# Recurrent attention and routed experts on one core: the state in compact form, its turning and routing rearranged

## The chip, the cores and the metric

The kernel runs on one core of a Trainium2 chip. The metric is the time of one execution on the device in microseconds (us). A core has five engines, each with a queue of its own that it works off in order: TensorE (PE, with its weight loads PEld), VectorE (DVE), ScalarE (ACT), GpSimd (POOL) and SyncE (SP), which issues DMAs. Engines wait for each other by semaphores.

## The reference

There are two parts. The first is a recurrence over 768 steps for each of 4 x 8 heads of width 40. The second sends each of the 3072 rows to one of 8 experts, by a hash of its token.

```python
for t in range(S):
    y[:, :, t] = einsum('bhd,bhde->bhe', rt, state)
    Sa = einsum('bhde,bhe->bhd', state, at)
    state_decay = state * wt[:, :, None, :] - einsum('bhd,bhe->bhde', Sa, bt)
    state = state_decay + einsum('bhd,bhe->bhde', vt, kt)
x = y.transpose(0, 2, 1, 3).reshape(3072, 320)
expert_idx = token_ids * 2654435761 % 8
out[mask_e] = maximum(x[mask_e] @ w1[e], 0) @ w2[e]
```

All is in fp32.

## The kernel before

**Tiling.** The sequence is cut into 12 chunks of 64 steps. A tile u is one chunk n of one group g of two batches with their 8 heads, so there are 24 tiles, u = 2 n + g. Inside a chunk the recurrence is solved with matrices: the products of a, b, k, r with running products of the decays w, and the inverse of a triangular matrix. Two halves of 64 partitions hold two heads (`par`) or the two batches (`be`), and four pairs of heads (`hp`) lie side by side. `quarters()` runs over hp, par and be, 16 matmuls in all, most of them of 64x64.

**Order.** `at_tick(tick, step)` collects every step as a function with a due time, in ticks; `STEPS` gives the fraction of a tick to the named steps. The plan is sorted by due time and issued in that order under a manual schedule, so each engine's program follows it. In tick T the kernel finishes tile T - 8 (`tile_b`, t0 = u + 8) and prepares tile T (`tile_a`). Ticks 8 to 31 are thus the main part; from tick 24 on there is nothing left to prepare.

**One tick, in TensorE's order.** Names are those of the PSUM tiles in the profile.
- c: r1 by the inverse um; ScalarE copies it to cv. u: the lower block of the next tile's inverse. rc, in two parts: cv by r and v by r, which VectorE masks into mr; between them nc, which turns cv; ScalarE copies it into `x_all`.
- z: turns the decayed b and k of tile T; ScalarE copies it to z_t. s: the state, in which two products with `ident` bring the old state in and 16 products add the chunk; VectorE multiplies the sum by the chunk's decay `pend` into sc, written twice (once for each head of a pair, with zeros in the other half, so that 128 rows hold a pair).
- a: the products of a with b and k; ScalarE copies them to nk and its lower part once more (L546). sd: turns sc; ScalarE copies it. x: the first half of the lower block of the inverse; ScalarE copies it to xi.
- r (r0, the state by a), t (at_t, which turns a of the next tile), r (r1, v by the masked products), y (state by r and z by mr; VectorE multiplies by the decays py into xs, and GpSimd's queue stores xs to x_rows), and t again (rv, which turns r and v).

**Groups.** For four tiles at a time VectorE inverts the 32x32 diagonal blocks (`group_i`): it transposes nk to nb, does 31 pairs of operations (L600 and L603, "outer" and "ub"), and transposes the result to ut (L608) and ug (L614). ScalarE fills ub at the start (L582).

**Decays.** For four tiles at a time `decays` builds the running products of w: clamp, chains on GpSimd, own, an exchange over TensorE, ends, a reciprocal, two spreading multiplies, transpositions pt and qt, and `pend`.

**PSUM.** `psum` hands out two large buffers in turn (tags psa0 and psa1), `bank` two small ones (psb0, psb1); ub takes the rest. A step that asks for a buffer waits until the buffer's last reader is done.

**Routing and experts.** `routing()` is a generator whose pieces are due every 0.42 tick from tick 11.5 on: it loads the token ids, counts and ranks them on VectorE, scatters token numbers to their slots (24 indirect DMAs by GpSimd), reads the slots back (idx_all, five DMAs by SyncE) and bounds them (src_all). After the last tick come the experts: gathers of x_rows, two matmul layers, scatters to out.

Of the kernel before, what the change touches and what calls it, by code (L numbers as in the profile page):

```python
# [18 lines left out]
def kernel(  # L19
# [98 lines left out]
    taken = [0, 0]  # L118

    def turn_of(i):  # L120
        taken[i] += 1
        return taken[i] % 2
# [25 lines left out]
    STEPS = ["c", "u", "rcc", "nc", "rcv", "z", "s", "a", "sd", "x", "r0", "at_t", "r1", "y", "rv"]  # L148
# [39 lines left out]
    x_all = hold.tile([P, 3, 2, HP, P], F32, name="x_all")  # L188
# [4 lines left out]
    sd_r = ring("sd", NG, [R, 2, HP, 2, D], all_of)  # L193
    sc_r = ring("sc", NG, [R, 2, HP, 2, C], all_of)
    pend_r = ring("pend", NR, [P, RN, NG, 2, HP, 2], all_of, NR)
    nk = hold.tile([P, LAG, 2, 2, HP, C], F32, name="nk")
    xi_r = ring("xi", 1, [P, H, C])
# [9 lines left out]

    @at_tick(-8.95)
    def _():
        for be in range(2):  # L210
            rows = slice(be * C + BLK, (be + 1) * C)
            nc.scalar.copy(xi_r(0)[rows, :, BLK:C], ident[rows, rows].unsqueeze(1).to_broadcast([BLK, H, BLK]))
# [30 lines left out]

    def paced(dma):

        dep = mybir.DependencyInfo(mybir.DependencyClass.Sync, mybir.DependencyReason.SCHED_ONLY)
        tc.add_manual_dep(dma.ins, pe_last[0].name, dep)
# [32 lines left out]
    def decays(ri, t_load, t_clamp, t_chain, t_own, t_ex, t_ends, t_pair, t_recip, t_en, t_spread, t_turn):  # L280
# [3 lines left out]
        chain = nc.vector if fast else nc.gpsimd  # L284

        for i in range(4 * RN):
            @at_tick(t_load + (0.06 * i if ri > 2 else 0))
            def _(i=i):
# [6 lines left out]
                eng = nc.scalar if fast and n % 2 else nc.sync  # L295
                r0 = (y * RN + n) * NG * H
                dma = eng.dma_start(x["pb"][r0:r0 + NG * H], src)
# [11 lines left out]
        def own():  # L309
            p, q = segs(x["pb"]), segs(x["qb"])  # L310
            x["own"] = own = work.tile([P, SEG, D], F32, tag="own", name="own", bufs=2)
            nc.vector.tensor_tensor(own[:], p[:, :, SL - 1], q[:, :, SL - 1], op=OP.mult)
            for s in range(SEG - 2, -1, -1):
                nc.vector.tensor_tensor(own[:, s], own[:, s], own[:, s + 1], op=OP.mult)
# [17 lines left out]
        def ends():  # L332
            ends = x["ends"]
            nc.vector.tensor_tensor(ends[:, 0:SEG], x["own"][:], ends[:, SEG].unsqueeze(1).to_broadcast([P, SEG, D]), op=OP.mult)
# [103 lines left out]
        def _():  # L438
# [3 lines left out]
            for par in range(2):  # L442
                rows = half(par)
                for be in range(2):
                    nc.scalar.copy(t[rows, :, :, be, :, par],
                                   p[rows].rearrange("p (be y n g hp two) -> p be y n g hp two", be=2, y=2, n=RN, g=NG, two=2)[:, be, 0, :, :, :, par])

    def tile_a(u):
# [19 lines left out]
        else:  # L468
            t_in, t_inz, t_mul, t_mulz = u - 1.36, u - 1.1, u - 0.6, u - 0.55
            t_z, t_at, t_a = (u - i + STEPS.index(n) / len(STEPS) for i, n in ((0, "z"), (1, "at_t"), (0, "a")))  # L470
            if u == LAG:
                t_at, t_mul, t_mulz, t_z, t_a = u + 0.66, u - 0.36, u + 0.225, u + 0.55, u + 0.79
# [59 lines left out]
        def _():  # L532
# [9 lines left out]
            if u > GRP - 2:  # L542
                nc.scalar.copy(both, p[:])  # L543
                for be in range(2):
                    low = slice(be * C + BLK, (be + 1) * C)
                    nc.scalar.copy(nk[low, u % LAG, :, 0, :, 0:BLK], p[low, :, 0:HP * C].rearrange("p two (hp t) -> p two hp t", hp=HP)[..., BLK:])  # L546
# [24 lines left out]
    def group_i(gi, t0, t1, t2, t3):  # L571
# [39 lines left out]
        def _():  # L611
            ub = x["u"]
            x["ug"] = ug = work.tile([P, BLK, BLK], F32, tag="ug", name="ug", bufs=1)
            nc.vector.transpose(ug[:].rearrange("p g t -> p t g"), ub[:].rearrange("p s t -> p t s"))  # L614
# [5 lines left out]
    def tile_m(u, t0):  # L620
# [5 lines left out]
        def _():  # L626
# [7 lines left out]
            for be in range(2):  # L634
                low = slice(be * C + BLK, (be + 1) * C)
                nc.scalar.copy(xi[low, :, 0:BLK], p[low])

        @at_tick(t0 - 1, "u")
        def _():
            ug, xi = groups[gi]["ug"], x["xi"]  # L640
            p = bank([P, H, BLK], "u_ps")
            for hp, par, be in quarters():
                h = hx(par, hp)
                low = slice(be * C + BLK, (be + 1) * C)
                mm(p[half(be), h, :], xi[low, h, :], ug[low, ti * H + h, :])
            x["um"] = um = work.tile([P, H, C], F32, tag="um", name="um", bufs=1)
            nc.scalar.copy(um[:, :, BLK:C], p[:])

        @at_tick(t0 - 0.7 if u else t0 - 0.93)
        def _():  # L650
            nc.scalar.mul(x["um"][:, :, 0:BLK], groups[gi]["ug"][:, ti * H:(ti + 1) * H, :], first[:, 0:1])

    def tile_s(u, t0):
# [5 lines left out]
        def in_rv(i):  # L659
            kind, be = divmod(i, 2)  # L660
            if i == 0:
                x["r"], x["x"] = r_r(u), x_all[:, u % 3]
# [3 lines left out]
        for i in range(4):  # L666
            @at_tick(5.0 + 0.2 * u if u < 2 else t0 - 1.84 + 0.09 * i)
# [12 lines left out]
        def _():  # L680
            x["rt"] = rv[:, :, 0]
            p = psum("t_ps")
# [548 lines left out]
```

## Time and profile before

| what | value |
|---|---|
| three runs, median (lowest, highest) | 708.71 us (699.46, 709.13) |
| the profiled execution | 702.85 us, its span 701.1 us |
| busy: PE, DVE, POOL, ACT | 606.5, 357.3, 269.2, 262.8 us |
| experts, from 432 us on | 269.0 us, PE busy 246.59 |
| L600 and L603, the pairs of the inversion | 62.7 and 65.0 us, 186 each |
| L738 mr, x24 | 1218 ns each |
| L765 sc, x22 | 819 ns each |
| L499 on POOL, 128x320, x40 | 872 ns each |
| L910 scatters to slots, x24 | 1027 ns each |

The busy time of an engine is a sum over the whole span. A line of the chain or of the timeline has the start, the duration, the engine and what ran; in the timeline the bracket at the end has the idle time ahead of the instruction and what ended it. A fp32 matmul appears as two records.

### The profile page before, as it was taken

Reading aid. Unit: us, or ns where it says so; the run is one execution under the profiler, and the core shown is the slowest. Engines: PE = TensorE matmul, PEld = TensorE weight load, DVE = VectorE, ACT = ScalarE, POOL = GpSimd, SP = SyncE. Lnnn points to the kernel's source line nnn. Section 1 sums busy time; section 2 is a strip of 40 time slices with the busy share of each in tenths; the row PEclk is TensorE's granted clock in tenths of the full one; section 3 lists DMA queues with packets and bytes.
Section 4 is the critical chain, followed back from the end, with each engine's and each line's share of the span. In section 5 each row is a group of like instructions: output and inputs, shape, how many; then the busy total and the mean of one; then the engine's idle time right before and its main releaser. Section 6 shows DMA issues by size and latency. Waiting matters only on the chain.

```text
span 701.1 us, 23965 instructions
## 1 busy us (share of the span) xinstructions
PE 606.5 (87%) x10442; PEld 455.0 (65%) x10442; DVE 357.3 (51%) x759; ACT 262.8 (37%) x520; POOL 269.2 (38%) x343
## 2 busy tenths in 40 slices
PE   0446678989999999989989994899999999999995
PEld 0335657877878888878878884364656556565653
DVE  6969797858988966873676313328111111111110
ACT  2576434754566657555534541111111111111110
POOL 2569367574637785454331111312213030210101
PEclk9988568997999999998989998699999999999999
DMA  9874053554555756774434522896322442120000
GB/s 136 157 114 113 2 105 78 116 123 91 110 110 114 133 101 102 131 136 66 80 55 82 117 55 73 297 339 217 102 73 87 145 149 85 46 93 20 28 5 29
DMA packets 163517, 73.86 MB, mean 105 GB/s; under 512 B 136078, under 2 KB 157135, under 8 KB 163408
## 3 DMA queue, kind: packets, MB, share of 16 engines
q1 hardware_dynamic: 153232, 55.55, 36.6%
q0 software_dynamic: 5824, 15.75, 8.4%
q10 hardware_dynamic: 4352, 0.98, 1.2%
q8 instruction: 83, 1.36, 0.9%
q14 instruction: 26, 0.21, 0.1%
HBM read 56.73 MB, written 12.16 MB: 98 GB/s over the span
## 4 chain that ended last, share of the span: by engine, by line
PE 39%; issue 33%; DVE 12%; POOL 6%; DMA 5%; SPq 2%; ACT 1%; POOLq 0%; DVEq 0%; ACTq 0%
PE r_ps L242 5%; PE y_ps L242 5%; PE s_ps L242 5%; PE rc_ps L242 4%; PE u_ps L242 4%; DVE ub L603 3%; DVE outer L600 3%; POOL out_dram L1030 3%; PE sd_ps L562 3%; PE a_ps L242 2%; PE z_ps L562 2%; POOL xg L1000 2%; PE t_ps L567 2%; PE nc_ps L747 2%; PE x_ps L242 2%
## 5 line engine op out<-in xcount | busy, mean ns | idle before, releaser
L1040 PE MATMUL dn_ps<-w,ht 128*128 128x320 f32 x384 | 104.9, 433 | 0.0
L1030 POOL DMA_INDIRECT out_dram<-o,idx_all x26 | 25.7, 990 | 185.4 <-ACT o L1029 178.6
L1020 PE MATMUL up_ps<-xt,w 128*128 128x416 f32 x256 | 94.0, 520 | 0.0
L1040 PEld LDWEIGHTS dn_ps<-w,ht 128*128 128x128 f32 x384 | 72.8, 190 | 32.1 <-issue 2.4
L1020 PEld LDWEIGHTS up_ps<-xt,w 128*128 128x128 f32 x256 | 47.5, 191 | 46.0 <-issue 46.0
L785 POOL DMA_DIRECT2D x_rows<-xs x44 | 24.5, 561 | 115.6 <-DVE xs L782 77.1
L603 DVE TENSOR_TENSOR ub<-ub,outer 128x31 f32<-128x31 f32 (+15 forms) x186 | 65.0, 349 | 6.3
L600 DVE TENSOR_TENSOR outer<-ub,nb 128x31 f32<-128x31 f32 (+15 forms) x186 | 62.7, 337 | 7.4 <-ACT ub L583 2.8
L1023 DVE TENSOR_SCALAR ht<-up_ps 128x416 f32<-128x416 f32 x32 | 18.9, 591 | 92.4 <-PE up_ps L1020 92.4
L1006 DVE COPY xt<-xg_ps 128x384 f32<-128x384 f32 x24 | 12.1, 551 | 83.4 <-PE xg_ps L1005 83.4
L562 PE MATMUL z_ps<-ident,z_all 128*128 128x128 f32 x192 | 32.0, 318 | 24.0 <-POOL z_all L499 10.7
L1029 ACT COPY o<-dn_ps 128x320 f32<-128x320 f32 x24 | 10.2, 426 | 101.6 <-PE dn_ps L1040 101.6
L738 DVE TENSOR_TENSOR mr<-rc_ps,after 128x1024 f32<-128x1024 f32 x24 | 29.2, 1218 | 29.3 <-PE rc_ps L242 29.3
L562 PEld LDWEIGHTS z_ps<-ident,z_all 128*128 128x128 f32 x192 | 24.9, 162 | 27.8 <-POOL z_all L499 11.9
L499 POOL TENSOR_TENSOR z_all<-z_all,qt 128x320 f32<-128x320 f32 x40 | 34.4, 872 | 13.0 <-DMA z_all<-in_k_dram 9.1
L687 ACT COPY rv<-t_ps 128x1024 f32<-128x1024 f32 x24 | 24.3, 1012 | 39.6 <-PE t_ps L567 39.6
L1025 ACT ACTIVATE ht<-up_ps 128x416 f32<-128x416 f32 x32 | 15.9, 514 | 60.8 <-PE up_ps L1020 60.8
L1000 POOL DMA_INDIRECT xg<-x_rows,src_all x26 | 25.5, 982 | 32.3 <-PE xg_ps L1005 17.5
L242 PE MATMUL u_ps<-ug,xi 32*64 32x32 f32 x768 | 30.6, 228 | 5.5 <-issue 2.7
L749 ACT COPY x_all<-nc_ps 64x512 f32<-64x512 f32 x44 | 25.6, 581 | 25.0 <-PE nc_ps L747 24.5
L543 ACT COPY nk<-a_ps 128x1024 f32<-128x1024 f32 x21 | 21.3, 1013 | 33.8 <-PE a_ps L242 33.4
L1016 PE MATMUL up_ps<-xt,w 64*128 64x416 f32 x128 | 28.4, 562 | 6.3 <-DVE xt L1006 3.9
(186 smaller groups left out, 1192.2 us busy)
## 6 DMA issues: line engine op xcount, KB each, us to landing
w<-in_moe_w_dram SPq DMA_DIRECT2D x7, 1280.0 KB, 7.1
w<-in_moe_w_dram SPq DMA_DIRECT2D x7, 1024.0 KB, 5.4
r<-in_r_dram SPq DMA_DIRECT2D x48, 80.0 KB, 3.9
x_all<-in_v_dram SPq DMA_DIRECT2D x48, 80.0 KB, 2.9
py<-p_rows POOLq DMA_DIRECT2D x24, 160.0 KB, 3.3
wt<-in_w_dram SPq DMA_DIRECT2D x24, 160.0 KB, 7.3
z_all<-in_b_dram SPq DMA_DIRECT2D x46, 80.0 KB, 2.9
z_all<-in_k_dram SPq DMA_DIRECT2D x46, 80.0 KB, 3.3
```

Of the source, the lines that this page charges most:

```text
L242: pe_last[0] = nc.tensor.matmul(out_, lhsT=lhsT, rhs=rhs, start=start, stop=stop, skip_group_check=True).ins
L499: eng.tensor_tensor(t, t, by.rearrange("p (h e) -> p h e", e=D), op=OP.mult)
L562: pe_last[0] = nc.tensor.transpose(dst, src, ident[:]).ins
L600: nc.vector.tensor_tensor(tv, ub[:, 0:j + 1, j:j + 1].to_broadcast([P, j + 1, m]), nb[:, j, j + 1:].unsqueeze(1).to_broadcast([P, j + 1, m ...
L603: nc.vector.tensor_tensor(o, o, tv, op=OP.add)
L738: nc.vector.tensor_tensor(t[:].rearrange("p two h t -> p (two h) t"), p[:].rearrange("p two (h t) -> p (two h) t", t=C), after[:].unsqueez ...
L749: nc.scalar.copy(x["x"][half(be), be], p[half(be)])
L1000: g = nc.gpsimd.indirect_dma_start(out=xg[:, 0:DM], out_offset=None, in_=x_rows[:], in_offset=bass.IndirectOffsetOnAxis(ap=idx, axis=0))
L1016: nc.tensor.matmul(banks[-1][:], lhsT=w1(f, 2), rhs=xt[part(f), 2, 0:n], start=True, stop=False)
L1020: nc.tensor.matmul(p[:], lhsT=w1(f, c), rhs=xt[:, c, 0:n], start=False, stop=(c == 1))
L1030: st = nc.gpsimd.indirect_dma_start(out=out[:], out_offset=bass.IndirectOffsetOnAxis(ap=idx, axis=0), in_=o[:], in_offset=None, bounds_che ...
L1040: nc.tensor.matmul(p[:], lhsT=ht[:, f, j * P:(j + 1) * P], rhs=w2(f), start=(f == 0), stop=(f == FP - 1))
```

## The change

- The state sc is kept once per head, without zeros. s has no products with `ident`; VectorE adds the old state to the sum (into `so`, which shares the one buffer of xs), and GpSimd multiplies by `pend` at t0 + 0.55.
- sd is 16 products of 40 columns, st by `ident`, with two copies. r0 and y's state part are quarters: 16 products instead of 8, into a large PSUM buffer. r0 keeps its buffer until rv (`kept`), so that at_t, y and rv use the other one in turn. For the first two tiles r0 and y's state part fall away.
- The order of steps has r0 right after a, sd after at_t, and r1 after y.
- u computes the upper 32 rows only, into um; um is built once per group by the transposition that made ug, and ScalarE's product with `first` is done once per group, at t3 + 0.02.
- nk's second copy reads nk instead of PSUM. x_all has two buffers instead of three, and v is loaded later.
- own and ends are done by GpSimd from the third round of decays on.
- Routing's first 14 pieces are due every 0.1 tick from tick 25.0, the others every 0.14 from 26.4.

```diff
     def turn_of(i):
-        taken[i] += 1
+        if i or kept[0] is None:
+            taken[i] += 1
+        else:
+            taken[i] = kept[0] + 1
         return taken[i] % 2
-    STEPS = ["c", "u", "rcc", "nc", "rcv", "z", "s", "a", "sd", "x", "r0", "at_t", "r1", "y", "rv"]
+    STEPS = ["c", "u", "rcc", "nc", "rcv", "z", "s", "a", "r0", "x", "at_t", "sd", "y", "r1", "rv"]
-    x_all = hold.tile([P, 3, 2, HP, P], F32, name="x_all")
+    x_all = hold.tile([P, 2, 2, HP, P], F32, name="x_all")
-    sd_r = ring("sd", NG, [R, 2, HP, 2, D], all_of)
-    sc_r = ring("sc", NG, [R, 2, HP, 2, C], all_of)
+    sd_r = ring("sd", NG, [R, 2, HP, D], all_of)
+    sc_r = ring("sc", NG, [R, 2, HP, C], all_of)
...
+        eng = nc.vector if ri < 2 else nc.gpsimd
-            nc.vector.tensor_tensor(own[:], p[:, :, SL - 1], q[:, :, SL - 1], op=OP.mult)
+            eng.tensor_tensor(own[:], p[:, :, SL - 1], q[:, :, SL - 1], op=OP.mult)
...
-                    nc.scalar.copy(nk[low, u % LAG, :, 0, :, 0:BLK], p[low, :, 0:HP * C].rearrange("p two (hp t) -> p two hp t", hp=HP)[..., BLK:])
+                    nc.scalar.copy(nk[low, u % LAG, :, 0, :, 0:BLK], nk[low, u % LAG, :, 0, :, BLK:])
...
-            x["ug"] = ug = work.tile([P, BLK, BLK], F32, tag="ug", name="ug", bufs=1)
-            nc.vector.transpose(ug[:].rearrange("p g t -> p t g"), ub[:].rearrange("p s t -> p t s"))
+            x["um"] = um = work.tile([P, BLK, C], F32, tag="um", name="um", bufs=2)
+            nc.vector.transpose(um[:, :, BLK:].rearrange("p g t -> p t g"), ub[:].rearrange("p s t -> p t s"))
+        @at_tick(t3 + 0.02, order=9)
+        def _():
+            um = x["um"]
+            nc.scalar.mul(um[:, :, 0:BLK], um[:, :, BLK:], first[:, 0:1])
...
-                mm(p[half(be), h, :], xi[low, h, :], ug[low, ti * H + h, :])
-            nc.scalar.copy(um[:, :, BLK:C], p[:])
-        @at_tick(t0 - 0.7 if u else t0 - 0.93)
-        def _():
-            nc.scalar.mul(x["um"][:, :, 0:BLK], groups[gi]["ug"][:, ti * H:(ti + 1) * H, :], first[:, 0:1])
+                mm(p[top, h, :], xi[low, h, :], um[low, ti * H + h, BLK:])
+            for be in range(2):
+                top = slice(be * C, be * C + BLK)
+                nc.scalar.copy(um[top, ti * H:(ti + 1) * H, BLK:], p[top])
...
-            @at_tick(5.0 + 0.2 * u if u < 2 else t0 - 1.84 + 0.09 * i)
+            @at_tick(5.0 + 0.2 * u if u < 2 else t0 - 1.84 + 0.09 * i if i < 2 else t0 - 1.53 + 0.09 * (i - 2))
...
             p = psum("t_ps")
+            kept[0] = None
...
-                    mm(p[half(be), c0:c0 + 2 * D], x["at_t"][0:R, be, hp, :], st[:, be, hp, :, 0:D],
+                x["r1_ps"] = p = psum("r1_ps")
+                kept[0] = taken[0]
+                for hp, par, be in quarters():
+                    mm(p[half(be), par, hp * D:(hp + 1) * D], x["at_t"][half(par), be, hp, :], st[half(par), be, hp, 0:D],
...
+                if n and i == 0:
+                    behind(pe_last[0], turned_state[0])
...
-                for par in range(2):
-                    mm(p[half(par)], ident[half(par), half(par)], sc[half(par), :, :, par, 0:D], stop=False)
+                x["so"] = so = work.tile([P, 2, HP, D], F32, tag="xs", name="so", bufs=1)
+                    nc.vector.tensor_tensor(so[:], sum_, st[:, :, :, 0:D], op=OP.add)
+            @at_tick(t0 + 0.55)
+                nc.gpsimd.tensor_tensor(st[:, :, :, 0:D], x["so"][:], pend.unsqueeze(3).to_broadcast([P, 2, HP, D]), op=OP.mult)
...
-            p = bank([P, DM], "y_ps")
+            p = psum("y_ps")
+            if n:
+                for hp, par, be in quarters():
+                    mm(p[half(be), par, hp * D:(hp + 1) * D], x["rt"][half(par), 1 - be, hp, :], sd[half(par), be, hp, :],
...
-                p = psum("sd_ps")
+                p = bank([P, 2 * HP, D], "sd_ps")
-                        whole(p[:, be, hp * R:(hp + 1) * R], sc[:, be, hp].rearrange("p two x -> p (two x)"))
+                            mm(p[half40(par), be * HP + hp, :], st[half40(par), be, hp, 0:D], ident[half40(par), half40(par)])
...
-        at_tick(11.5 + 0.42 * i, order=7)(lambda: next(steps, None))
+        at_tick(25.0 + 0.1 * i if i < 14 else 26.4 + 0.14 * (i - 14), order=7)(lambda: next(steps, None))
```

## The prediction

> **What bounds the kernel now.** I read the busy times first: TensorE 87% of 701.1 us, every other engine at 51% or less. The table by stage puts TensorE at some 95% of the time between 124 and 337 us (201.95 of 213), the part in which the 24 tiles run one after the other, one "tick" each. So I went to the chain that ended last, inside one undisturbed tick (columns: start, us, what):
>
> ```profile
> 260.44 1.77 PE s_ps L242 x36
> 262.21 1.09 PE a_ps L242 x64
> 263.30 1.02 PE sd_ps L562 x8
> ...
> 267.30 1.61 PE y_ps L242 x48
> 268.91 0.71 PE t_ps L567 x16
> 269.62 0.62 PE c_ps L242 x32
> 270.25 1.05 PE u_ps L242 x32
> 271.30 0.62 PE rc_ps L242 x32
> ```
>
> Piece follows piece with no gap: a tick is 13.71 us of TensorE (s at 260.44 and again at 274.15), all matmuls. The question is what stands just behind them. ScalarE, in the timeline of the same tick:
>
> ```profile
> 263.63 1.01 ACT L543 COPY nk<-a_ps 128x1024 f32<-128x1024 f32 x1 [2.04 <-PE a_ps L242]
> 264.68 0.74 ACT L546 COPY nk<-a_ps 32x256 f32<-32x256 f32 x2
> ...
> 266.91 0.60 ACT L516 ACTIVATE at_t<-t_ps 128x512 f32<-128x512 f32 x1
> ```
>
> From nk to at_t ScalarE has no pause: it is 3 to 4 us behind TensorE, and today nobody waits for that. The second place is seen in the chain of the last tick, which has no u:
>
> ```profile
> 424.94 0.73 PE t_ps L567 x16
> ...
> 427.30 1.21 PE rc_ps L242 x63
> ```
>
> t ends at 425.67 and rc starts 1.63 later, after the two copies rv and cv on ScalarE. In the tick above, c and u (0.62 + 1.05) last 1.67: u just covers these copies. VectorE's timeline, in two ticks:
>
> ```profile
> 262.99 1.97 DVE L614 STREAM_TRANSPOSE ug<-ub 128x1024 f32<-128x1024 f32 x1
> ...
> 278.91 2.17 DVE L590 STREAM_TRANSPOSE nb<-nk 128x1024 f32<-128x1024 f32 x1 [2.12 <-ACT nk L546]
> ```
>
> ug starts at the end of s and lasts 2 us; nb waits for ScalarE. In that second tick xs starts 1.9 us after y ended and costs nothing. And the end of routing, SyncE's issues and then VectorE:
>
> ```profile
> 376.57 0.69 SPq L917 DMA_DIRECT2D idx_all<-slot_tokens x1
> 377.32 4.27 SPq L919 DMA_DIRECT2D idx_all<-slot_tokens x4
> ```
> ```profile
> 383.08 0.18 DVE L923 TENSOR_SCALAR src_all<-idx_all 128x26 int32<-128x26 int32 x1 [1.77 <-DMA idx_all<-slot_tokens]
> ```
>
> From the first idx load to src_all it is 6.5 us.
>
> **What the Trainium skill says.** "TensorEngine Tiling (Array Packing)", section Performance Considerations: packing speeds up TensorE, not the emptying of PSUM, which may become the bottleneck. The trace agrees: c's 32 records on four 64x64 tiles take 0.62 us, their copy 0.59. "PSUM — Partial Sum Buffer", section Engine vs sequencer instructions: ScalarE, VectorE and GpSimd are strict first in, first out; so one waiting instruction holds all behind it. "SBUF — State Buffer", section SBUF: two separate sides: GpSimd and VectorE lock a shared port pair for a whole instruction. The trace fits: ends (L334) takes 2.56 us at 180.11 beside GpSimd, 0.29 at 80.42. "TensorE: Matmul & The Clock Gate", section Step-by-step: loading weights scales with their columns; x (32 columns, two tiles) has 0.62 for 32 records, r1 (64 columns, two tiles) 1.06.
>
> **The change, part by part.** Sums are against the profiled execution (702.85 us, span 701.1); the median of the three runs, 708.71, is 0.8% above it.
>
> *TensorE's arithmetic.* s loses its identity products (0.70 of 1.77). u falls from 1.05 to about 0.62, as x has the same 32x32 form. r0 in four tiles takes 0.62 instead of 0.70, y about 1.65 instead of 1.61. sd turns 40 columns in two tiles: between 0.62 (x) and 1.06 (r1); I take 0.70. Left alone this is some 1.5 us per tick, 36 us over all.
>
> *What takes its place in a tick.* (a) rc waits for cv: 1.65 after t's end, before 1.68. u's gain is gone. (b) r0 holds one of the two large PSUM buffers until r1, so at_t, y and the next t share the other: y waits until ScalarE has read at_t. From the start of a: nk at +1.33 (mean of seven ticks), 1.05 to the next copy, the two low copies now from SBUF at about 0.42 (xi from SBUF in L212: 0.40), 0.86 with gaps, xi 0.77, at_t 0.60: y starts at +4.67, though TensorE could at +3.65. Then y 1.65 and r1 1.06: t starts at +7.38, before at +6.70. (c) s is shorter by 0.70, but a waits for the copy z_t, 1.12 after s starts: -0.60. Sum: 0.68 - 0.03 - 0.60 = +0.05. Bounds -0.4 to +0.4, by the copies' size. Over 14 full ticks (10 to 23): +1. The low copies' new source frees a's buffer after nk alone, at +2.38; at_t's transpositions, due at +2.36, get it in time. The sd copies, two of 40x320 at about 0.43 each, end before r1 comes.
>
> *The group's um.* Its product with first now stands in ScalarE's queue ahead of nk. It waits for the transposition um on VectorE, behind so: end of s + 0.05 + 0.49 (as xs) + 1.96, then about 1.15 for 128x1024 from SBUF (128x512 from PSUM takes 0.59, 1024 1.01). nk starts 2.3 later, and all behind it, y too. Ticks 10, 14, 18, 22: +9. Bounds 0 (if something else is later there) and 12.
>
> *ub.* Its copies (1.03 + 0.19) stand between r and rv. With y between r1 and t they were free; now r1 is last, so rv, cv and rc come 1.05 later in the same four ticks: +4.
>
> *nb.* In ticks 11, 15, 19, 23 nb and five pairs of the inversion come before xs: nb from a's start +3.2 (the low copies' end) to +5.4, the first five pairs 2.7 (343.89 to 346.35 holds four larger ones in 2.46), xs 0.49, until +8.7. t now needs y's buffer, free at +8.7 instead of +7.38: 1.3 each, +5. The shorter add (about 0.5 instead of 0.82) doesn't help behind nb's wait.
>
> *own, ends to GpSimd; routing away.* The waits they cause today go: ticks 11, 13, 14 lie 2.8, 1.7, 3.1 over 13.71, and the chain there holds the wait for tok, ends with 2.47 and ovt with 2.41: -7.5 (bounds -3, -9). GpSimd's own 1.5 and ends 0.55 per round, by its 0.55 for 128x160, and 0.87 for the new multiply, fit beside its 38%; the multiply comes most of a tick before r0 and sd read the state.
>
> *The front.* Two r0 and y's first parts go, but nk of tile 7 queues behind um's product and with it the exchange and ends that GpSimd's spreading needs: 0, bounds -6 and +4.
>
> *The last ticks.* Without z and a a tick has 11.07. rc again waits; s loses 0.70 but waits for x_all (1.19 after nc, of which rcv covers 0.62); with the shorter sd about -0.5. Against it: VectorE in tick 25 was busy 10.15 of 11.5; minus a pair and the lighter add, plus 7.3 of routing by its own rows, 17.4: so holds the bank that sd needs, xs the buffer of t. Tick 25 ends +6 later. Tick 26 has um's product ahead of xi and of the sd copies that r1 waits for, +1.3 net. Then 24 scatters of 1.27 (1.03 and a gap) fill GpSimd until about 6.5 us into tick 29; 3.3 for the last to land (median 4.2 from issue), 6.5 for idx, 1.4 for the small steps, and xs of tick 29, queued behind src_all, comes near +18 where y ended at +8.8: t 8 later. tok, the empty slots and the five idx loads move along in SyncE's queue: v of tile 23 stands behind idx and lands some 20 us after tick 29 began, a few us before r1 of the next tick asks for it. In tick 25 the wait for tok (2.2 today) lies early, before mr is due, and is not counted; it would add up to 2. Ticks 27, 28, 30: -1.6. Sum: +14 (bounds -3 and +20).
>
> Total: 1 + 9 + 4 + 5 - 7.5 + 0 + 14 = +25.5, 728 us in the terms of the profiled run. Expert layers are untouched.
>
> **The rivals.** *R1, TensorE's saving counts.* If the waits (b), um, nb and those of the last ticks are mostly covered, 25 of the 36 us come, and 3 from routing: 675. For it: TensorE is gapless for 300 us. Against it: 1.63 in the last tick, and ScalarE without pause. This ends on the other side; it decides if y starts at a's start +4.0 or earlier. *R2, a draw.* Middle ticks as I have them, but the last ticks absorb routing (VectorE is only 2.54 busy of 11.1 in tick 28) and um and ub cost 5 instead of 13, as the waits overlap: 702.85 + 1 + 5 + 5 - 7.5 = 706. Against it: routing's small operations stand in tick 25, not in tick 28. *R3, worse.* so and xs share one buffer; if GpSimd is late, so waits for the rows' store and TensorE for both, 1 us in 20 ticks: 748. For it: GpSimd's rows already wait on xs in 13 ticks; against it: the store is issued 5 us before the next so.
>
> **How the numbers follow.** The forecast 0.50, R3 0.13, R2 0.23, R1 0.14. The forecast's own range is 712 to 742; the range 693 to 750 adds R2 and R3 and leaves R1's core out. A change below 2% of this kernel is about what can't be told from none. Faster by over 2% 0.13, within 0.24, slower 0.63.
>
> **What would show it.** Right: rc waiting for ScalarE's cv in every tick; y for at_t; in four ticks nk behind um with a gap over 2 us; t behind xs in ticks 11, 15, 19, 23; ticks 25 and 29 near 17 and 19 us. Wrong: middle ticks under 13.2 us, or last ticks all near 10.5. sd shows its own price: 0.7 or 1.06.

## The result, and the profile after

The changed kernel takes 773.38 us (median of four runs, 769.7 to 773.81) against 705.25 us (699.46 to 709.13) for the kernel before: ratio 1.096, 95% interval 1.086 to 1.106. The prediction was 728 us, range 693 to 750: the direction was right, the size was not.

Time by stretches of the recurrence, read from the start of each tick's c products in the two timelines, one execution each (us):

| stretch | before | after | difference | predicted |
|---|---|---|---|---|
| ticks 10 to 23 | 216.5 | 252.1 | +35.6 | +11.5 |
| ticks 24 to 30 | 80.8 | 117.6 | +36.8 | +14 |
| the rest (front, tick 31, experts) | 403.8 | 401.9 | -1.9 | 0 |

In the page of the changed kernel TensorE is busy 646.7 us, where it was 606.5, although the products were made smaller. The row for the granted clock says why (tenths of full speed in 40 slices; first after, then before):

```profile
PEclk9968579687667797876766556659999999999998
```
```profile
PEclk9988568997999999998989998699999999999999
```

From slice 6 to slice 26 the clock of the kernel before is mostly full; that of the changed one goes up and down between half and full. The table by stage gives the mean as 0.94 before and 0.75 after in ticks 10 to 23, and 0.96 and 0.61 in ticks 24 to 30 (the columns are stretch, length, busy times of PE, PEld, DVE, ACT and POOL, then the clock, the DMA share and GB/s; the kernel before first):

```profile
128.30:344.80 216.50, 205.33 (x5569) 176.05 (x5566) 157.92 (x325) 128.71 (x238) 124.18 (x153) 0.94 0.58 109
344.80:425.60 80.80, 77.68 (x2172) 68.36 (x2171) 41.10 (x84) 35.74 (x66) 18.45 (x30) 0.96 0.39 75
```
```profile
127.20:379.30 252.10, 225.76 (x6290) 199.60 (x6289) 141.05 (x289) 133.21 (x255) 118.84 (x159) 0.75 0.45 94
379.30:496.90 117.60, 103.14 (x2541) 92.80 (x2540) 42.19 (x109) 38.01 (x75) 41.54 (x57) 0.61 0.36 52
```

Most of the waits that the prediction named are there. TensorE's timeline in tick 16, the counterpart of the gapless tick of before:

```profile
247.64 0.63 PE L240 MATMUL r_ps<-sc,at_t 64*64 64x40 f32 x32
248.19 0.69 PE L240 MATMUL x_ps<-ut,nk 32*32 32x32 f32 x32
249.00 0.63 PE L564 MATMUL t_ps<-ident,at 128*128 128x128 f32 x4
249.56 0.81 PE L240 MATMUL sd_ps<-ident,sc 40*40 40x40 f32 x32
251.18 0.78 PE L240 MATMUL y_ps<-sd,rv 64*64 64x40 f32 x32 [0.81 <-ACT at_t L518]
251.89 1.93 PE L240 MATMUL y_ps<-z_all,mr 128*64 128x40 f32 x32
253.75 1.93 PE L240 MATMUL r_ps<-x_all,nk 64*64 64x40 f32 x32
```

y waits 0.81 for ScalarE's copy of at_t. But look at the next two lines: y's second part and r1 take 1.93 each, 60 ns per record, where the tick in the kernel before had 35 ns. After the pause TensorE runs at half clock. In a group's last tick TensorE stops earlier and for longer, as ScalarE's um product stands ahead of nk, and at_t needs the buffer that nk reads (whole timeline, tick 18; nk ends at 283.42). The profile calls this stop "issue", which is its word where it finds no semaphore:

```profile
281.38 1.15 ACT L621 ACTIVATE um<-um,first 128x1024 f32<-128x1024 f32 x1 [2.46 <-DVE um L616]
282.43 0.99 ACT L545 COPY nk<-a_ps 128x1024 f32<-128x1024 f32 x1
...
283.53 0.63 PE L564 MATMUL t_ps<-ident,at 128*128 128x128 f32 x4 [1.81 <-issue]
```

And in the last ticks TensorE stops in the middle of a group of products, again with no semaphore that the profile could name. This is tick 28, while GpSimd issues the 24 scatters (417.9 to 471.2 us), then VectorE behind it; a stop of 3.62 us in tick 29 begins after the last scatter:

```profile
458.68 0.40 PE L240 MATMUL y_ps<-sd,rv 64*64 64x40 f32 x8
462.87 0.87 PE L240 MATMUL y_ps<-sd,rv 64*64 64x40 f32 x22 [3.79 <-issue]
```
```profile
465.70 0.49 DVE L790 TENSOR_TENSOR xs<-y_ps,py 128x320 f32<-128x320 f32 x1 [8.29 <-PE y_ps L240]
```

The end of routing came as the prediction had it, though the time it cost there is small. SyncE's issues in tick 29, then VectorE and TensorE:

```profile
477.19 0.37 SPq L927 DMA_DIRECT2D idx_all<-slot_tokens  x1
477.61 3.85 SPq L929 DMA_DIRECT2D idx_all<-slot_tokens  x4
```
```profile
484.69 0.18 DVE L933 TENSOR_SCALAR src_all<-idx_all 128x26 int32<-128x26 int32 x1 [9.02 <-DMA idx_all<-slot_tokens]
...
485.79 0.47 DVE L790 TENSOR_TENSOR xs<-y_ps,py 128x320 f32<-128x320 f32 x1
```
```profile
486.32 0.70 PE L569 MATMUL t_ps<-ident,r 64*128 64x64 f32 x8 [0.87 <-DVE xs L790]
```

xs stands behind src_all, which waits 9 us for the slots, and t comes after xs. But r1 ended only at 485.45, so that t is 0.87 late and not 8.

So these waits are about as long as foreseen or shorter, and most of the time is lost around them. What decides the clock is the question of the experiments.

### The profile page after: what moved, and what is told of

It reads as the page before. It is cut to its first block, busy times and chain, and to the rows that moved or that the text cites. A ratio compares the mean times of both kernels' runs of the same rounds, so it can differ in the third digit from the quotient of the medians.

```text
span 771.6 us, 26198 instructions
## 1 busy us (share of the span) xinstructions
PE 646.7 (84%) x11522; PEld 498.9 (65%) x11522; DVE 336.8 (44%) x739; ACT 269.7 (35%) x546; POOL 288.6 (37%) x379
## 4 chain that ended last, share of the span: by engine, by line
issue 29%; PE 12%; POOL 6%; DVE 3%; DMA 1%; ACT 1%; SPq 1%; POOLq 0%; DVEq 0%; ACTq 0%
POOL out_dram L1040 3%; POOL xg L1010 3%; PE y_ps L240 2%; PE rc_ps L240 2%; PE r_ps L240 1%; PE s_ps L240 1%; PE t_ps L569 1%; PE c_ps L240 1%; PE nc_ps L756 1%; PE u_ps L240 1%; DMA slot_tokens<-token,key_i 1%; PE sd_ps L240 1%; DVE outer L602 0%; DVE mr L747 0%; DMA idx_all<-slot_tokens 0%
## 5 line engine op out<-in xcount | busy, mean ns | idle before, releaser
L1033 DVE TENSOR_SCALAR ht<-up_ps 128x416 f32<-128x416 f32 x32 | 18.9, 591 | 93.0 <-PE up_ps L1030 93.0
L564 PE MATMUL z_ps<-ident,z_all 128*128 128x128 f32 x192 | 36.6, 352 | 22.9 <-POOL z_all L501 11.5
L1016 DVE COPY xt<-xg_ps 128x384 f32<-128x384 f32 x24 | 12.1, 551 | 83.3 <-PE xg_ps L1015 83.2
L564 PEld LDWEIGHTS z_ps<-ident,z_all 128*128 128x128 f32 x192 | 29.2, 183 | 26.8 <-POOL z_all L501 12.7
L1039 ACT COPY o<-dn_ps 128x320 f32<-128x320 f32 x24 | 10.2, 426 | 101.6 <-PE dn_ps L1050 101.6
L240 PE MATMUL y_ps<-z_all,mr 128*64 128x40 f32 x768 | 38.8, 275 | 2.9 <-issue 1.0
L240 PE MATMUL r_ps<-x_all,nk 64*64 64x40 f32 x768 | 39.7, 277 | 0.5 <-issue 0.3
L501 POOL TENSOR_TENSOR z_all<-z_all,qt 128x320 f32<-128x320 f32 x40 | 34.1, 864 | 15.6 <-DMA z_all<-in_k_dram 15.4
L790 DVE TENSOR_TENSOR xs<-y_ps,py 128x320 f32<-128x320 f32 x24 | 11.7, 488 | 62.6 <-PE y_ps L240 37.7
L240 PEld LDWEIGHTS y_ps<-z_all,mr 128*64 128x64 f32 x768 | 35.2, 187 | 4.9 <-issue 1.5
L240 PEld LDWEIGHTS r_ps<-x_all,nk 64*64 64x64 f32 x768 | 36.3, 190 | 2.3 <-issue 0.5
L722 ACT COPY r<-r_ps 128x320 f32<-128x320 f32 x24 | 10.3, 429 | 77.6 <-PE r_ps L240 77.6
## 6 DMA issues: line engine op xcount, KB each, us to landing
w<-in_moe_w_dram SPq DMA_DIRECT2D x7, 1280.0 KB, 11.2
```

Source lines behind the costliest of these rows:

```text
L240: pe_last[0] = nc.tensor.matmul(out_, lhsT=lhsT, rhs=rhs, start=start, stop=stop, skip_group_check=True).ins
L501: eng.tensor_tensor(t, t, by.rearrange("p (h e) -> p h e", e=D), op=OP.mult)
L564: pe_last[0] = nc.tensor.transpose(dst, src, ident[:]).ins
L1033: nc.vector.tensor_scalar(ht[:, f, 0:n], p[:], 0.0, None, op0=OP.max)
```

## The experiments

Ratios, with 95% intervals, are against the kernel before on the same chip. "Half clock" is the time at a granted clock of 0.5 in the record of the clock. Times of ticks are those of one traced execution each.

### First theories: a pause, the work, or the routing

Theory 1: pauses lower the clock. Theory 2: waits and work add up at a clock that doesn't depend on them. Theory 3: the routing's move is the main cost.

**The pause filled with small products.** The sd products of a tick are issued twice:

```diff
-                for be in range(2):
+                for be in (0, 1, 0, 1):
                     for hp in range(HP):
                         for par in range(2):
                             mm(p[half40(par), be * HP + hp, :], st[half40(par), be, hp, 0:D], ident[half40(par), half40(par)])
```

> The changed kernel with its sd products issued twice in each tick (32 more records of 40x40, the same values into the same tile), so that some 0.6 us of work stands where TensorE waits about 0.8 us for the at_t copy. Theory 1 (a pause of TensorE of 0.8 us lowers its granted clock for the next 7 to 13 us, and this is the larger part of the loss): the wait ahead of y shrinks to 0.3 us or less, the mean clock of the attention rises, and the time falls by 10 to 35 us from 773 although work was added. Theory 2 (the clock is low for other reasons, and only waits and work add up): at least 773, up to 790 where sd's copy comes late for r1. Theory 3 (the routing in the last ticks is the main cost): 773 within 4 us.

Measured: 794.14 us, 1.122 (1.113 to 1.131). From 150 to 300 us the clock did rise, 0.73 to 0.87, but the last ticks lost more than that:

```profile
400.00:450.00 50.00, 43.55 (x872) 38.43 (x872) 14.69 (x40) 12.11 (x23) 18.59 (x23) 0.50 0.32 49
450.00:500.00 50.00, 45.63 (x1000) 40.27 (x997) 6.29 (x13) 13.71 (x27) 17.11 (x24) 0.50 0.37 36
```

For 100 us TensorE is busy some 90% of the time and stays at half clock. A gate that only looked at busy time would have opened. Theory 1 as it stood can't explain this.

**A pause put into the kernel before.** The first r1 product waits for ScalarE's at_t copy of the same tick:

```diff
...
+                if u > 1 and (hp, par, be) == (0, 0, 0):
+                    dep = mybir.DependencyInfo(mybir.DependencyClass.Sync, mybir.DependencyReason.SCHED_ONLY)
+                    tc.add_manual_dep(pe_last[0], at_copy[0].name, dep)
```

> The kernel before with one dependency added: from tick 10 on the first r1 product of each tick waits for ScalarE's copy of the at_t turned in that tick, a pause of about 1.2 us in some 14 ticks. Nothing else is changed. Theory 1 (pauses lower the clock): the granted clock of ticks 10 to 23 falls from 0.9 to 1.0 to 0.65 to 0.8, and the time rises by 40 to 70 us to 745 to 775. Theory 2 (only the waits add up): +10 to +20 us, 715 to 725, clock as before. Theory 3 says nothing of this run other than theory 2 does.

Measured: 715.76 us, 1.014 (1.005 to 1.023). The pauses are there, in 14 ticks (the waits of TensorE: us in total, times, longest):

```profile
PE r_ps L242 <- ACT at_t L518: 14.3, 14, 1.2
```

The clock stayed at 0.933 over the span; half clock in ticks 10 to 23 was 13.7 us, less than the 23.9 of the kernel before. A pause of 1 us in every tick is thus not enough by itself: theory 1 falls. Something else must differ between the two kernels around the pause.

**at_t ahead of r0.**

```diff
-    STEPS = ["c", "u", "rcc", "nc", "rcv", "z", "s", "a", "r0", "x", "at_t", "sd", "y", "r1", "rv"]
+    STEPS = ["c", "u", "rcc", "nc", "rcv", "z", "s", "a", "at_t", "x", "r0", "sd", "y", "r1", "rv"]
```

> The changed kernel with the order of steps a, at_t, x, r0, sd, y in place of a, r0, x, at_t, sd, y: at_t's products take the large buffer that z left, r0 the one that a's copy leaves, and y no longer comes 0.8 us behind at_t's copy; instead r0 waits some 0.3 to 0.5 us for the nk copy. Theory 1 (pauses lower the clock): the pause becomes shorter, the mean clock of the attention rises by 0.05 or more, 735 to 760. Theory 2 (waits only): 0.3 to 0.5 us in 14 ticks, 766 to 770. Theory 3: 770 to 774.

Measured: 802.7 us, 1.132 (1.124 to 1.139). The expectation was wrong in all theories: r0 did not wait for nk, but for the at_t copy as y had done, and for longer:

```profile
PE r_ps L240 <- ACT at_t L518: 28.7, 14, 3.7
```

Half clock in ticks 10 to 23 rose from 124.3 to 154.9 us. It says nothing on the theories, but gives longer pauses to learn from.

**Routing at its old ticks.**

```diff
-        at_tick(25.0 + 0.1 * i if i < 14 else 26.4 + 0.14 * (i - 14), order=7)(lambda: next(steps, None))
+        at_tick(11.5 + 0.42 * i, order=7)(lambda: next(steps, None))
```

> The changed kernel with the routing's steps due at the ticks of the kernel before (11.5 + 0.42 per step), nothing else changed. Theory 1 (pauses in every tick): ticks 25 to 29 fall from 18.3, 14.5, 22.1, 18.8, 18.9 us to about 11 to 15 each, some 20 to 30 us, but the middle ticks lose 0 to 15 by the scatters among them: 745 to 770. Theory 3 (the routing's move is the main cost): 715 to 735, near the kernel before. Theory 2: 750 to 760, the sum of the waits in ticks 25 to 29 only.

Measured: 759.26 us, 1.068 (1.059 to 1.077), 14 less than the changed kernel. Ticks 24 to 30 fall from 117.6 to 88.9 us, and ticks 10 to 23 rise from 252.1 to 265.2. Theory 3 (715 to 735) falls: the routing is one part of the loss. Its move cost 29 where it was put. What it saved where it was taken away is less sure: 13 here, and 21 between two later runs (226.5 and 247.3), while in two other runs that leave ticks 10 to 23 as they are these took 245.2 and 261.7.

### A new theory: the share of the array

In all traces the granted clock changes only at multiples of 3.413 us, between two values. That is what the Trainium skill says in "TensorE: Matmul & The Clock Gate", section What's actually happening: a gate with two ratios, 4/8 and 8/8, set by how busy TensorE was in a free-running window of some 3.4 us. The section HAM oscillation adds that idle gaps of more than some 3.4 us make it fall again; the pause here has 0.8. Both speak of busy time. Take the same tick in such windows:

```profile
241.37:244.78 3.41, 3.41 (x71) 2.84 (x64) 0.58 (x2) 1.67 (x4) 2.96 (x4) 0.50 0.70 131
244.78:248.20 3.42, 3.40 (x136) 3.07 (x134) 3.28 (x8) 1.32 (x2) 2.70 (x6) 1.00 0.33 90
248.20:251.61 3.41, 2.48 (x101) 2.12 (x100) 2.73 (x7) 3.31 (x8) 0.19 (x1) 1.00 0.51 94
251.61:255.02 3.41, 3.41 (x74) 3.25 (x68) 1.03 (x3) 0.25 (x1) 0.28 (x1) 0.50 0.31 64
255.02:258.44 3.42, 3.42 (x86) 3.11 (x84) 2.73 (x7) 1.96 (x3) 1.37 (x3) 0.50 0.63 131
258.44:261.85 3.41, 3.41 (x84) 2.81 (x84) 0.00 (x0) 1.65 (x6) 1.84 (x3) 0.50 0.49 111
261.85:265.26 3.41, 3.39 (x124) 3.04 (x120) 2.92 (x6) 1.96 (x5) 2.37 (x3) 1.00 0.34 51
```

In the window with the pause TensorE was busy 2.48 of 3.41, and the next one has half clock. Then come two windows that are busy for 100%, and each is followed by half clock again; the third, just as busy, is followed by full. So I counted something else: for each record its streamed columns (40 in a timeline's 64x40), times rows x columns that it uses of the array (its 64*64) over 128 x 128, the most that occurs, with 2048 such columns as one unit. (A product counts twice, as it appears as two records; a transposition by `whole` or `turn` appears as one.) That the clock follows this count is theory 4. The seven windows hold 0.83, 1.34, 0.45, 0.47, 0.57, 0.70 and 1.36 units. Over the first six traces (both kernels and the four runs above) the best single limits were 0.51 at full clock and 0.69 at half clock. With these two numbers fixed, the ten later runs give, for the windows between 75 and 490 us:

| clock in a window | units in it | windows | next one at half | next one at full |
|---|---|---|---|---|
| full | below 0.51 | 98 | 94 | 4 |
| full | 0.51 or more | 673 | 17 | 656 |
| half | below 0.69 | 322 | 309 | 13 |
| half | 0.69 or more | 115 | 10 | 105 |

Busy time can't do this at half clock: of 524 windows in all runs that were busy for over 98%, 190 were followed by full clock; 170 of these are among the 180 with 0.69 units or more. Nor can streamed columns alone: with limits fitted on the same six traces they are wrong in 70 of the later windows at full clock and in 100 of those at half, where rows x columns is wrong in 21 and 23. Columns weighted by rows alone do as well at full clock (22) and not at half (64).

The same count for one tick tells what the change did: before it held 4.66 units, after 3.72. The sd turning went from 0.50 to 0.06, r0 and y's state part from 0.31 to 0.16 each, s lost the 0.16 of its identity products, u 0.03. A full tick is four windows. r0, x, sd and y's state part now stand within 4 us of each other, with the new pause among them and only at_t's four products dense. From tick 24 on, without z, a and at_t, 2.47 units are left (3.41 before). At half clock such a tick takes some 17 us, five windows of 0.49 on average. It seldom reaches 0.69.

**The pause filled with dense work.** As long as the doubled sd products, but on the whole array:

```diff
                 p = bank([P, 2 * HP, D], "sd_ps")
+                for i in range(5):
+                    whole(p.rearrange("p h d -> p (h d)")[:, 0:P], ident[:])
```

> The changed kernel with five transpositions of the 128x128 identity issued ahead of the sd products of each tick into the same tile, which the sd products then overwrite: some 0.68 us of TensorE work per tick, as long as the doubled sd products of the run before were, in the same pause, but on the whole array in place of 40 x 40 of it. Theory 4 (new: the granted clock is decided in stretches of 3.41 us by how much of the array the products occupy, rows x columns x streamed columns: in the runs so far it fell where the share sum of a stretch was below about 0.51 and came back where it was above about 0.69; the change took 0.94 of 4.66 such units from each tick): the five add 0.31 to the stretch that falls, the mean clock of ticks 10 to 24 rises from 0.73 to 0.85 or more, and the time falls to 725 to 760 although 15 us of work were added. Theory 1 (only the length of a pause counts): the same as with the doubled sd products, about 794. Theory 2 (waits and work alone): 773 to 790.

Measured: 771.71 us, 1.086 (1.079 to 1.092). Half clock in ticks 10 to 23 fell from 124.3 to 49.2 us, and these ticks took 234.1 us, 18 less than in the changed kernel and 15 less than with small products (248.8, 90.6 at half clock). The five stream half as many columns as the doubled sd products, 640 against 1280. The last ticks, with the scatters, were at half clock for 111.3 of 133.4 us and took the gain back. The theory is right on the middle ticks; its total was wrong. By its count five are too few for the last ticks: 2.78 units, some 0.56 in each of five windows.

**Sixteen dense products, or the sd products five times, in ticks 24 to 30 alone.** No wait is concerned here; the two differ in how much of the array is used.

```diff
+                for i in range(16 if u > 14 else 0):
+                    whole(p.rearrange("p h d -> p (h d)")[:, 0:P], ident[:])
```
```diff
-                for be in range(2):
+                for be in (0, 1) * (5 if u > 14 else 1):
```

> The changed kernel; in ticks 24 to 30 alone (no z, a and at_t products any more, 2.47 units of the array per tick) sixteen dense 128x128 transpositions go ahead of the sd products: 2.2 us at full clock, 1.0 unit. Theory 4 (array share, two thresholds): ticks 24 to 30 of the changed kernel took 15.5, 18.3, 14.5, 22.1, 18.8, 18.9 and 9.5 us because at half clock no stretch of 3.41 us reaches 0.69; with the sixteen one does in most ticks, so that ticks 28 and 29 fall to 13 to 16 us although each has 2.2 us more to do, and the seven ticks together change by -10 to +5. Theory 1 and 2: ticks 28 and 29 become 21 to 23, together +15 to +28.

> The changed kernel; in ticks 24 to 30 alone the sd products are issued five times over: 2.4 us more at full clock, as the sixteen dense ones, but only 0.24 unit of the array. Theory 4: no stretch reaches 0.69, the clock stays at half and the added work costs 4.5 us per tick: ticks 28 and 29 take 22 to 25, the seven ticks together +20 to +35. Theory 1 and 2: the same as with the dense ones.

Measured: 779.98 us (773.99 and 785.97) and 794.98 us, 1.123 (1.113 to 1.134). Ticks 24 to 30 took 118.5 and 146.9 us, against 117.6 without any addition. Windows of tick 28, dense first (its trace is of the execution that took 785.97 us):

```profile
467.93:471.34 3.41, 3.41 (x18) 3.26 (x16) 0.00 (x0) 0.73 (x2) 1.70 (x2) 0.50 0.79 84
471.35:474.76 3.41, 3.27 (x121) 2.95 (x120) 0.00 (x0) 0.84 (x2) 0.00 (x0) 1.00 0.12 11
474.76:478.17 3.41, 1.34 (x35) 1.15 (x37) 0.49 (x1) 0.44 (x2) 0.65 (x2) 1.00 0.00 0
```
```profile
475.27:478.69 3.42, 3.21 (x96) 3.06 (x92) 0.00 (x0) 0.45 (x2) 0.00 (x0) 0.50 0.00 0
478.69:482.10 3.41, 2.20 (x48) 2.12 (x50) 0.00 (x0) 0.39 (x1) 0.00 (x0) 0.50 0.02 5
```

The window full of dense transpositions (0.96 units) is followed by full clock; the one full of small sd products (0.21 units, busy for 3.21) is not. Some 14 us of dense work (1.96 a tick at full clock) cost 1 us, some 17 us of small work cost 29, though it streams 2.5 times as many columns. Half clock fell from 90.8 to 57.5 us with the dense work and rose to 115.4 with the small. Stops explain 5 us of the difference (TensorE stood 11.6 and 16.7 us). That separates theory 4 from theories 1 and 2. But ticks 28 and 29 did not fall to 13 to 16 us as expected (19.7 and 20.3): in the third window shown TensorE stood for 2.07 of 3.41 us, and the clock fell again.

**sd in the kernel before as 64x64 products.**

```diff
-                        whole(p[:, be, hp * R:(hp + 1) * R], sc[:, be, hp].rearrange("p two x -> p (two x)"))
-                nc.scalar.copy(sd[:].rearrange("p b h two x -> p (b h two) x"),
-                               p[:].rearrange("p b (h x) -> p (b h) x", x=C)[:, :, 0:D])
+                        for i in range(2):
+                            mm(p[half(i), be, hp * R:hp * R + C], sc[half(i), be, hp, i, :], ident[half(i), half(i)])
+                for i in range(2):
+                    nc.scalar.copy(sd[half(i), :, :, i], p[half(i)].rearrange("p b (h x) -> p b h x", x=R)[:, :, :, 0:D])
```

> One part of the change done alone in the kernel before: its eight 128x128 sd transpositions (1.09 us, 0.50 units of the array per tick) replaced by the 16 diagonal 64x64 products that carry the state (about 0.4 us, 0.125 units), and ScalarE's copy in two halves; no product waits for anything new by design, the result is the same. Theory 4: the units per tick fall from 4.66 to 4.28, more stretches fall below 0.51, the mean clock of the attention falls from 0.93 to 0.75 to 0.88, and the time rises by 5 to 40 us although 0.7 us of work per tick were taken out. Theory 1 and theory 2: 0.6 to 0.7 us off in 22 ticks, 690 to 700, clock as before.

Measured: 721.59 us, 1.015 (1.008 to 1.021). My price was wrong: sixteen products are 32 records and took 1.15 us, not 0.4, and hold 0.25 units. So no work was taken out. Half clock fell to 10.2 us in ticks 10 to 23 and rose to 20.5 in ticks 24 to 30. The fall of the middle ticks' clock that theory 4 asked for did not come; the run is slower, and it doesn't decide. What did grow are TensorE's stops called issue, from 5.4 us in 6 times to 12.1 in 21 in ticks 10 to 23.

**Dense products in the kernel before** (the same five, ahead of its sd):

```diff
                 p = psum("sd_ps")
                 sc = sc_r(g)
+                for i in range(5):
+                    whole(p[:, 0, 0:R], ident[:])
```

> The kernel before with the same five dense transpositions ahead of its sd products, 0.68 us more in each tick, TensorE being the bound. Theory 4: work of 15 us is added, and the falls of the clock in ticks 12 to 25 (some 20 us of loss) become fewer: 700 to 718. Theory 1 and 2: +13 to +16, 718 to 725, clock as before.

Measured: 715.74 us, 1.007 (1.001 to 1.013). Half clock over ticks 10 to 30 fell from 30.7 to 13.7 us, which pays for most of the added work. As theory 4 has it: 3.6 us more than the kernel before on this chip (712.18), where work alone asks for 13 to 16.

### The waits, priced

**ScalarE's um product 0.4 tick later.**

```diff
-        @at_tick(t3 + 0.02, order=9)
+        @at_tick(t3 + 0.4, order=9)
```

> The changed kernel with ScalarE's um product due 0.4 tick later, so that the nk copy of ticks 10, 14, 18 and 22 no longer stands behind it. Waits alone (the prediction's price): -9. Theory 4: ticks 10, 14, 18, 22 lose their falls (stretches of 0.15 to 0.31 units) and 2 to 3 us of half clock each besides: -12 to -25, 748 to 762. If the products u or c then wait for um instead: 773.

Measured: 750.81 us, 1.063 (1.055 to 1.071), 22.6 less than the changed kernel. In the changed kernel ScalarE's um product waits for VectorE for 10.0 us in four times, and TensorE's stops ahead of at_t in these four ticks are 2.54, 2.38, 1.81 and 2.33, 9.1 us in all. In this trace the wait of um is gone, one stop of 1.21 is left in these ticks, and half clock in ticks 10 to 23 falls from 124.3 to 60.7 us. The prediction had priced the stops at 9: their length was right, and what they cost with the clock was 2.5 times as much.

**um later, routing early, and v's part of rc ahead of cv's.** The first two as above, and

```diff
         @at_tick(t0, "rcc")
-                mm(p[half(be), par, c0:c0 + C], cv[half(par), hp, be, :], x["rt"][half(par), 1 - be, hp, :])
+                mm(p[half(1 - be), par, c0:c0 + C], rv[half(par), be, 1, hp, :], x["rt"][half(par), 1 - be, hp, :])
...
         @at_tick(t0, "rcv")
-                mm(p[half(1 - be), par, c0:c0 + C], rv[half(par), be, 1, hp, :], x["rt"][half(par), 1 - be, hp, :])
+                mm(p[half(be), par, c0:c0 + C], cv[half(par), hp, be, :], x["rt"][half(par), 1 - be, hp, :])
```

> The changed kernel with three of its waits taken away and no filling: ScalarE's um product 0.4 tick later, the routing at the ticks of the kernel before, and in each tick the rc products that read v ahead of those that read cv, so that cv's copy is covered. The pause of 0.8 us ahead of y stays. Single effects measured: um -22.6, routing -14. Theory 4 with the scatters as the second cause: the two add up and the swap gives 2 to 8 more, 725 to 742; ticks 10 to 23 still fall below 0.51 in about half of the ticks by the pause ahead of y, clock 0.80 to 0.90 there; the last ticks 11 to 14 us each. Waits alone: 773 - 9 - 14 - 4 = 746 or more.

Measured: 737.21 us, 1.044 (1.034 to 1.053). The two single effects add up to what was found (773.4 - 22.6 - 14.1 = 736.7; these are medians of different chips, and by the ratios 1.096 - 0.033 - 0.028 = 1.035 was to be expected). A gain by the swap isn't seen. The clock of ticks 10 to 23 did not come up to 0.80: it is 0.77, and half clock there is 116.1 us. Among TensorE's stops of that trace between 100 and 440 us are 9.5 us that the profile calls issue, with the scatters back in these ticks, and 6.9 us for at_t ahead of y.

**Dense filling, um later and routing early.**

> The same dense filling, with the routing at the ticks of the kernel before and ScalarE's um product due 0.4 tick later, so that nk no longer stands behind it. Theory 4: the clock of the middle ticks as in the dense filling or better, the last ticks not held at half clock: 705 to 735. Theory 1: 745 to 770. Theory 2: 745 to 765 (14 off for the routing, 5 to 9 for um, some added for the filling).

Measured: 738.84 us (725.12 to 747.86), which spreads too far for a ratio. In the profiled execution half clock in ticks 10 to 23 is 34.1 us, but ticks 24 to 30 have 75.1, and in ticks 10 to 23 TensorE stands for 34.4 us, 17.3 of it called issue. Next to the run without filling (737.21) it gains nothing.

**own and ends on GpSimd, alone in the kernel before** (from the third round of decays on):

```diff
+        by = nc.vector if ri < 2 else nc.gpsimd
...
-            nc.vector.tensor_tensor(own[:], p[:, :, SL - 1], q[:, :, SL - 1], op=OP.mult)
+            by.tensor_tensor(own[:], p[:, :, SL - 1], q[:, :, SL - 1], op=OP.mult)
...
-            nc.vector.tensor_tensor(ends[:, 0:SEG], x["own"][:], ends[:, SEG].unsqueeze(1).to_broadcast([P, SEG, D]), op=OP.mult)
+            by.tensor_tensor(ends[:, 0:SEG], x["own"][:], ends[:, SEG].unsqueeze(1).to_broadcast([P, SEG, D]), op=OP.mult)
```

> One part of the change done alone in the kernel before: own and ends of the later decay rounds on GpSimd in place of VectorE. The prediction's price for this and the routing's move together was -7.5. Here: -2 to -7 where VectorE's work ahead of mr or xs made TensorE wait (ex waits for own 2.5 in one tick), 0 or a few us more where GpSimd, slower, brings the next round's ex and ends late.

Measured: 700.25 us, 0.982 (0.973 to 0.991), a little more than expected. The trace, of a 703.53 us execution, has no gain where the prediction put it, in the middle ticks: they took 218.0 us (216.5 before). Tick 10 starts 3.7 us earlier; ahead of it ex waits for own 1.7 us in place of 6.4. With the rc products swapped as well:

> The kernel before with own and ends on GpSimd, as run alone before (0.982 of the kernel before), and the rc products that read v ahead of those that read cv. TensorE waited for cv 1.0 us in one tick of the kernel before only, so that the swap brings 0 to 3 us: 0.975 to 0.985 of the kernel before. Where mr, which comes from the last rc product, is late for y or where rv's copy is late for the v products: up to 0.99.

Measured: 700.1 us, 0.990 (0.986 to 0.993). Both are 1 to 2% faster than the kernel before. The swap adds nothing that can be told.

## Why the prediction was wrong in size

**A term was missing: the clock.** Every sum was made with durations at full clock. In ticks 10 to 23 the changed kernel had 124.3 us at half clock, the one before 23.9; in ticks 24 to 30 it is 90.8 against 6.8. At half clock a record of r1 takes 60 ns in place of 35, so 42% of such time is lost while TensorE is busy, which it was for about 90%: an estimate of 0.42 x 0.9 x 100.4 = 38 us in the middle ticks and 0.42 x 0.88 x 84 = 31 us in the last ones. The measured differences are 35.6 and 36.8. By this estimate all waits and all the work saved sum up to a few us only, where the prediction had +11.5 and +14.

**Step by step.**
- (b), y waits for at_t: right; up to 0.82 us in ten of ticks 10 to 23, 6.7 us in all.
- (a), rc waits for cv: seen at full clock (0.34 at 327.18), otherwise only in weight loads of rc, 1.7 us in seven times. At half clock c and u last 2.1 us (from 256.73), longer than the copies. No lever: a gain by the swap was not seen.
- um: the stops were right (9.1 us in four ticks), their price was not: +9 predicted, 22.6 measured. Of the terms that were measured alone, this is the one that the clock multiplies most.
- nb and xs: right in kind, t waits for xs 4.2 us in three ticks (11, 19, 23), +5 in four predicted. ub's copies stand between r and rv as said (1.01 at 291.03).
- sd: 32 records at 25 ns, 0.81 with the last one's end; the 0.70 taken was near.
- own, ends and routing away, -7.5: own and ends alone took some 8 us off the kernel before (medians), in the trace ahead of tick 10 and not in the middle ticks, and routing's move took some 13 to 21 off these. The sum was probably under-sized.
- The last ticks, +14: the step that failed besides the clock. Ticks 25 and 29 are 18.3 and 18.9 (17 and 19 said), and that is luck. In tick 25 sd waits for so 1.42 us, where the delay by VectorE was put at 6; 14.9 us of the tick are at half clock. In tick 29 xs starts 17.3 after the tick does (18 said), but t comes 0.87 late and not 8: y itself was late, by a stop of 3.62 us and 12.1 us at half clock. "Ticks 27, 28, 30: -1.6" is wrong by 20 us in ticks 27 and 28 alone: 22.1 and 18.8 us, where the kernel before had 11.2 and 11.1. TensorE stood 10.5 us in eight stops called issue, two of them 3.79 and 3.62 us in ticks 28 and 29, and the few units per tick kept the clock at half.

**The rivals.** R1 counted on the saving of work, but the clock lost with it cost more. R2 let the last ticks absorb the routing; they took 29 us less without it (88.9 against 117.6). R3 gave 748 by so waiting for the rows' store in 20 ticks; TensorE waits for so only in ticks 24 and 25, 2.2 us in all, behind other work of VectorE. None of the cases had a clock in it, though the Trainium skill's page names the gate and the trace of before shows half clock in ticks 12, 14, 17, 22 and 24, 30.7 us in all. I had read them as disturbances, and took an undisturbed tick as the rule.

## What to carry to other kernels

When TensorE is the bound, look at the granted clock by windows of 3.4 us before making its products smaller: here work that used less of the array ran slower, and taking away stops of 9 us in all brought 22.6. Count rows x columns x streamed columns per window for the stage as it will be, and where it comes near the limit take away waits before work. Dense filling kept the clock up in the middle ticks, but it did no more than pay for itself (771.71 and 738.84 us with it, 773.38 and 737.21 without). And keep loose work, such as scatters, out of the stage that has the least dense work left.

## What was not expected of the hardware

- The clock followed the share of the array used, with two limits (0.51 to fall, 0.69 to rise, in units of 2048 full-array columns per 3.413 us), not the time busy. It was fitted and tested on this kernel only; whether rows x columns is the exact measure stays open.
- TensorE stops for 0.3 to 3.8 us in the middle of a group of products, with no semaphore named ("issue"). The kernel before has five such stops over 0.25 us, 5.2 us, in the 137 us in which it issues its scatters, and none in the 100 us ahead. The changed one has seven, 6.9 us, in the 54 us of its scatters, and 2.4 us in the 287 us ahead (the stops behind nk apart).
- Sixteen fp32 products of 64x64 on two tiles cost as much as the eight transpositions of 128x128 that they stood for: 1.15 and 1.09 us.

A likely cause of many of these stops is in the traces: TensorE's own instructions. The page has a queue of that name (packets, MB, share; before, then after):

```profile
q8 instruction: 83, 1.36, 0.9%
q8 instruction: 91, 1.49, 0.8%
```

Its packets have 16 KB and grow with TensorE's records, weight loads included (20884 and 23044): some 65 bytes a record in both. In ticks 10 to 30 of the 16 traces 155 of 258 such stops end 1.1 to 1.9 us after the end of one of these packets, where some 41 would by chance (these stretches are 16% of the time); of 225 stops with a named cause 55 do. Among the 155 are the two long ones: packets ended at 461.31 and 479.30, and TensorE went on at 462.87 and 481.07. So TensorE seems to have waited for its next instructions, of which many small products need more. No run tested this, and why a packet comes late isn't shown.
